# The ordered list of an attention and MLP kernel: lambda on another queue, four weight slices converted later, weight stages filled at its end

## The chip, the cores and the metric

One core of one Trainium2 chip runs the whole program. The metric is device time in microseconds (us) of one execution; 649.22 us is the median of three runs of the kernel before (647.98 to 650.60).

## The reference, cut to what matters

The input is `q`, `k`, `v` of shape 2 x 8 x 768 x 64 and one decay `lam` per head. Attention is linear and decays with distance; it goes through the sequence in blocks and carries a 64 x 64 state per head:

```python
intra = (q_b @ k_b.T * lam**(i-j) for i>=j) @ v_b
inter = (q_b * lam**(i+1)) @ state
state = lam**block * state + (k_b * lam**(block-1-j)).T @ v_b
```

Its output, as 1536 tokens x 512, goes through two MLPs one after the other, each 512 -> 2048 -> 512: the first with h * tanh(softplus(h)) (Mish), the second with max(h, 0) squared.

## The kernel before, in words

Tokens are taken in four chunks t of 384 (N). A *pair* is two heads of one chunk, so there are 16 pairs i = 4t + p. For each pair, TensorE makes the scores (`S`), VectorE masks them with a table of decays (`P1`, `P0`, line L242), ScalarE scales k (`KD`, L203), GpSimd scales q (`QD`, L210), TensorE makes updates and outputs (`U`, `V`), VectorE advances the state (`A`, `A2`, L237), and the result leaves PSUM as a high part (`XH`, ScalarE, L268) and a low part (`XL`, VectorE, L272). The tables (`T`, L179 and L182) are made of `lam` by VectorE at the start. Pairs 2 and 4 to 15 share the PSUM banks X and Y, so the scores of one of them wait for the one ahead to leave.

The MLPs multiply in three passes of a high and a low part (`mm3`, L58 to L60). They run in 128 *steps*, 64 a layer. A step is one chunk t with one slice F of 128 of the hidden width: `m_h` (12 matmuls), the activation `e_a` (L308), its high and low part `e_hi` and `e_lo` (the last is GpSimd's `gl`, L326, once a step), and `m_y` (12 matmuls in layer 0, 9 wider ones in layer 1). Sixteen steps make a phase: four slices, for each of the four chunks.

Each slice F has two weight tiles (io = 0 for `m_h`, 1 for `m_y`), 64 *units* in all, in the order in which they are used, eight a phase. The weights arrive as 64-bit floats and are converted: load of 512 KB (`W`, SP's queue, five raw buffers), `cv_a` on ScalarE (`CA`, L93), three instructions of VectorE in `cv_b` (`CB0`, `CB1`, `CC`: L102, L104, L106), copy of the high part on ScalarE (`CH`, L117), low part on GpSimd (`CL`, L125). A converted tile lies in one of eight slots F mod 8, and `cv_h` refuses to write a slot whose tile has been used fewer than four times.

The attention and steps 0 to 15 (with `m_h(16)`) are not issued in program order. `plan()` writes down operations with an engine, an estimated duration, what they follow, and sometimes a due time; `issue()` runs a list schedule over them: of the operations that can start within 0.25 us of the earliest on an engine, the one with the earliest due time. The order that comes out is fixed at build time; on the chip each engine runs its own list in order and waits only for data. Sixteen units (slices F = 0 to 7) are in this list, and three more loads.

Behind the list the loop runs iterations s = 16 to 127. Each issues `m_h` up to step s+3, `e_c(s+1)`, in odd s one `conv()`, and `y_all(s)`. One `conv()` finishes one unit (`CH`, `CL`), takes the next through `cv_b`, the one after it through `cv_a`, and loads another. `weight()` calls `conv()` until a tile that is asked for is there.

Of the kernel before, what the change touches and what calls it, by code (L numbers as in the profile page):

```python
# [14 lines left out]
RING, RAW = 8, 5  # L15
GROUPS = ((0, 4), (4, 8), (8, 12), (12, 16)), ((0, 4), (4, 8), (8, 12), (12, 16))
AHEAD = 16
# [9 lines left out]
def tile_attn_mlp_mlp(ctx, tc, qkv_in, lam, w1i, w1o, w2i, w2o, out):  # L27
# [354 lines left out]
    ops = {}  # L382
# [13 lines left out]
    def plan():  # L396
        NI = NB * NP
        step_due = lambda s: STEP0 + STEP * s
        op("lam", "ACTq", 0.1, [], lambda: act.dma_start(
            out=lam_b, in_=bass.AP(lam.tensor, lam.offset, [[0, P], [1, H]])))  # L400
        op("lp", "DVE", 0.4, ["lam"], lam_pairs)
        for p in range(NP):
            op(f"T{p}", "DVE", 1.2, ["lp"], lambda p=p: tables(p))
        for i in range(NI):
            a = pr[i]
            j = i - 1
            op(f"kq{i}", "SP", 1.05, [f"kq{j}", f"S{i-4}", f"QD{i-4}"], lambda i=i: load_kq(i))
            op(f"kv{i}", "SP", 1.05, [f"kv{j}", f"kq{i}", f"V{i-4}"], lambda i=i: load_kv(i))
            S_prev = [f"XL{j}", f"A2{j}"] if i > NP else [f"XL{i-3}", f"A2{i-3}"] if i == 3 else []
            if i == NP:  # L410
                S_prev = ["XL2", "A22"]
            op(f"S{i}", "PE", 0.75, [f"kq{i}"] + S_prev + [f"S{j}"], a.scores)
            op(f"KD{i}", "ACT", 0.85, [f"kv{i}", f"T{a.p}"], a.scale_k)
            op(f"QD{i}", "POOL", 1.05, [f"kq{i}", f"T{a.p}", f"V{i-3}"], a.scale_q)
            op(f"U{i}", "PE", 0.4, [f"S{i}", f"KD{i}"], a.updates)
            op(f"P1{i}", "DVE", 0.56, [f"S{i}", f"T{a.p}", f"V{i-2}"], lambda a=a: a.mask(1))
            op(f"P0{i}", "DVE", 0.56, [f"P1{i}"], lambda a=a: a.mask(0))
            chain = [f"U{i}", f"V{i-2}", f"A2{i-2}"] + ([f"A2{i-4}"] if not a.first else [])
            if a.first:
                op(f"AC{i}", "ACT", 0.25, chain, lambda a=a: a.advance(0, a.u[0], (0,)))  # L420
                op(f"AD{i}", "DVE", 0.25, chain, lambda a=a: a.advance(0, a.u[0], (1,)))
                op(f"A{i}", "DVE", 0.56, [f"AC{i}", f"AD{i}"], lambda a=a: a.advance(1, a.u[1]))
            else:
                op(f"A{i}", "DVE", 1.12, chain, lambda a=a: [a.advance(c, a.u[c]) for c in range(2)])
            op(f"V{i}", "PE", 1.35, [f"P0{i}", f"A{i}", f"QD{i}", f"kv{i}"], a.outputs)
            own = step_due(i - 4.7) if i >= NP else None
            op(f"XH{i}", "ACT", 0.5, [f"V{i}"] + ([f"XH{j}"] if a.p else []), a.leave_hi)
            op(f"XL{i}", "DVE", 0.56, [f"XH{i}"], a.leave_lo, own)
            if not a.last:
                op(f"A2{i}", "DVE", 0.57, [f"V{i}", f"XL{i}"], a.leave_state, own)  # L430

        nu = 16
        for u in range(nu):
            F, io = units[u]
            op(f"W{u}", "SP", 1.4, [f"W{u-1}", f"CL{u-RAW}"], lambda u=u: cv_load(u))
            op(f"CA{u}", "ACT", 0.68, [f"W{u}", f"CA{u-1}", f"CC{u-2}"], cv_a)
            op(f"CB0{u}", "DVE", 0.45, [f"CA{u}", f"CC{u-1}"], lambda: cv_b(0))
            op(f"CB1{u}", "DVE", 0.72, [f"CB0{u}"], lambda: cv_b(1))
            op(f"CC{u}", "DVE", 0.72, [f"CB1{u}"], lambda: cv_b(2))
            op(f"CH{u}", "ACT", 0.66, [f"CC{u}", f"CH{u-1}"], cv_h)  # L440
            op(f"CL{u}", "POOL", 1.35, [f"CH{u}", f"CL{u-1}"], cv_l, None if F < 4 else step_due(3 + 1.6 * (u - 8)))
        for u in range(nu, nu + 3):
            op(f"W{u}", "SP", 1.4, [f"W{u-1}", f"CL{u-RAW}"], lambda u=u: cv_load(u), step_due(u - 4))
        unit = {units[u]: u for u in range(nu)}
        for s in range(AHEAD + 1):
            _, _, t, f, st, en = steps[s]
            w, wo = f"CL{unit[f, 0]}", f"CL{unit.get((f, 1))}"
            for a in range(KT):
                dep = [f"XL{NP*t+a}", w, f"MISH{s-2}" if a == 0 else f"HM{s}.{a-1}"]
                op(f"HM{s}.{a}", "PE", 0.53, dep, lambda s=s, a=a: m_h(s, [a]))  # L450
            op(f"MISH{s}", "ACT", 0.5, [f"HM{s}.{KT-1}"], lambda s=s: e_a(s))
            op(f"GH{s}", "ACT", 0.52, [f"MISH{s}", f"GH{s-1}", f"YM{s-2}.{KT-1}"], lambda s=s: e_hi(s))
            op(f"GL{s}", "POOL", 1.05, [f"GH{s}"], lambda s=s: e_lo(s), step_due(s) - 0.6)
            if s == AHEAD:
                break
            for e in range(KT):
                dep = [f"GL{s}", wo, f"YM{s}.{e-1}" if e else f"YM{s-1}.{KT-1}"]
                if st and t:
                    dep.append(f"YD{s-1}.{e}")
                if s == 0:  # L460
                    dep += ["XL0", "A20"] if e < 2 else ["XL1", "A21"]
                    dep += ["XL3", "A23"] if e < 2 else []
                op(f"YM{s}.{e}", "PE", 0.53, dep, lambda s=s, e=e: m_y(s, e), step_due(s) + 0.5 * e)
                if en:
                    op(f"YD{s}.{e}", "ACT", 0.5, [f"YM{s}.{e}"], lambda s=s, e=e: y_out(s, e), step_due(s + 1))

    def issue():
        names = list(ops)
        for n in reversed(names):
            o = ops[n]  # L470
            for a in o.after:
                x = ops[a]
                x.due = min(x.due, o.due - o.dur - LAT - (LAND if x.eng in ("SP", "ACTq") else 0))
        free = {}
        wait = dict(ops)
        trace = []
        while wait:
            cand = {}
            for n, o in wait.items():
                if all(ops[a].end is not None for a in o.after):  # L480
                    r = max([free.get(o.eng, 0.0)] + [
                        ops[a].end + (0 if ops[a].eng == o.eng != "SP" else LAT)
                        + (LAND if ops[a].eng in ("SP", "ACTq") and o.eng != "SP" else 0) for a in o.after
                    ])
                    cand.setdefault(o.eng, []).append((r, o.due, n))
            best = None
            for eng, c in cand.items():
                r0 = min(c)[0]
                pick = min((x for x in c if x[0] <= r0 + SLACK), key=lambda x: (x[1], x[0]))
                if best is None or pick[0] < best[0]:  # L490
                    best = pick
            r, _, n = best
            o = wait.pop(n)
            o.end = free[o.eng] = r + o.dur
            trace.append((r, n, o))
            o.emit()
        if PLAN:
            for r, n, o in trace:
                print(f"{r:7.2f} {o.end:7.2f} {o.eng:4} {n:8} due {o.due:6.1f}")

    with tc.manual_schedule():
        one = const.tile([P, 1], F32, name="one")
        pool.memset(one, 1.0)
        act.activation(gp.tile([P, N], F32, tag="u", name="table", bufs=4)[:, :1], one, AF.Mish)
        make_identity(nc, ident)

        zero = gp.tile([P, N], F32, tag="gl", name="zero")[:, :2 * P]
        dve.memset(zero, 0.0)
        warm = bank("X")
        for _ in range(WARM):  # L510
            pe.matmul(warm[:, :2 * P], lhsT=zero[:, :P], rhs=zero, start=True, stop=True)
        for z in state + mid:
            pool.memset(z, 0.0)
        TAGS = ("y0", "y1"), ("y2", "y3"), ("X", "Y"), ("y0", "y1")
        pr = [Pair(i, TAGS[i] if i < NP else ("X", "Y")) for i in range(NB * NP)]
        plan()
        issue()
        ahead = AHEAD


        wide.append(AHEAD)
        for s in range(AHEAD, len(steps)):
            layer, t, f, _, en = steps[s][1:]
            while ahead + 1 < len(steps) and ahead < s + LOOK:
                ahead += 1
                m_h(ahead)
                e_a(ahead)
            if s + 1 < len(steps):
                e_c(s + 1)
            if s % 2:  # L530
                conv()
            y_all(s)

            for k in range(KT):
                d = s - k - 1
                if d >= 0 and steps[d][1] == 0 and steps[d][5] and phases[steps[d][0]][3] == NF:
                    x_split(steps[d][2], k)
# [50 lines left out]
```

## Time and profile before

| | |
|---|---|
| median of three runs | 649.22 us |
| the profiled execution, its own time | 650.57 us |
| its span, first to last instruction | 648.4 us |
| mean granted TensorE clock | 0.979 |
| TensorE busy | 607.6 us (94%) |
| VectorE busy | 292.3 us (45%) |
| ScalarE busy | 231.4 us (36%) |
| GpSimd busy | 248.2 us (38%) |

Busy time of TensorE is taken from matmuls whose ends are modelled, so 94% is not its peak; whether work flows is better seen from the distance between equal steps. An arrow `<-` at the end of a row of a timeline names what ended the idle time that stands before it. Busy shares over the whole span mix two quite different stretches: the list (to about 146 us) and the loop.

### The profile page before, as it was taken

Reading aid. Unit: us, or ns where it says so; the run is one execution under the profiler, and the core shown is the slowest. Engines: PE = TensorE matmul, PEld = TensorE weight load, DVE = VectorE, ACT = ScalarE, POOL = GpSimd, SP = SyncE. Lnnn points to the kernel's source line nnn. Section 1 sums busy time; section 2 is a strip of 40 time slices with the busy share of each in tenths; the row PEclk is TensorE's granted clock in tenths of the full one; section 3 lists DMA queues with packets and bytes.
Section 4 is the critical chain, followed back from the end, with each engine's and each line's share of the span. In section 5 each row is a group of like instructions: output and inputs, shape, how many; then the busy total and the mean of one; then the engine's idle time right before and its main releaser. Section 6 shows DMA issues by size and latency. Waiting matters only on the chain.

```text
span 648.4 us, 9101 instructions
## 1 busy us (share of the span) xinstructions
PE 607.6 (94%) x3592; PEld 560.3 (86%) x3592; DVE 292.3 (45%) x483; ACT 231.4 (36%) x486; POOL 248.2 (38%) x229
## 2 busy tenths in 40 slices
PE   7888989999999989998999989998999989998997
PEld 6777878999999979998999869987899879987996
DVE  5999974201444334442445534442555445440223
ACT  3465633332333323333344434433233323332111
POOL 2376542121344323343455434334233424434122
PEclk8799989999999989999999979999899999999999
DMA  8865641000011121111222111111211122000112
GB/s 308 294 233 197 215 150 69 1 1 1 16 58 61 62 66 54 58 59 60 66 66 66 38 60 65 55 55 55 67 58 53 51 66 66 33 1 0 50 50 97
DMA packets 15737, 49.86 MB, mean 77 GB/s; under 512 B 1872, under 2 KB 1872, under 8 KB 15696
## 3 DMA queue, kind: packets, MB, share of 16 engines
q1 hardware_dynamic: 15552, 49.29, 22.3%
q8 instruction: 28, 0.46, 0.3%
q14 instruction: 13, 0.11, 0.0%
q10 hardware_dynamic: 144, 0.00, 0.0%
HBM read 46.14 MB, written 3.15 MB: 76 GB/s over the span
## 4 chain that ended last, share of the span: by engine, by line
PE 48%; POOL 3%; issue 3%; DVE 0%; ACT 0%; POOLq 0%; ACTq 0%
PE y L59 9%; PE y L60 8%; PE y L58 8%; PE h L60 4%; PE h L58 4%; PE h L59 4%; PE Y L60 2%; PE Y L58 2%; PE Y L59 2%; POOL w L125 2%; PE X L60 1%; PE X L58 1%; PE X L59 1%; POOL gl L326 1%; DVE y L359 0%
## 5 line engine op out<-in xcount | busy, mean ns | idle before, releaser
L326 POOL TENSOR_TENSOR gl<-g,gh 128x384 fp32r<-128x384 f32 x64 | 67.0, 1046 | 180.8 <-ACT gh L319 175.9
L326 POOL TENSOR_TENSOR gl<-u,gh 128x384 fp32r<-128x384 f32 x64 | 67.7, 1059 | 168.8 <-ACT gh L316 98.4
L359 DVE TENSOR_TENSOR y<-y,y 128x384 f32<-128x384 f32 (+1 forms) x84 | 50.3, 612 | 122.2 <-PE y L60 122.0
L58 PE MATMUL h<-xh,w 128*128 128x384 f32 x288 | 98.3, 341 | 0.1
L60 PE MATMUL h<-xh,w 128*128 128x384 f32 x288 | 97.3, 338 | 0.5 <-POOL w L125 0.5
L59 PE MATMUL h<-xl,w 128*128 128x384 f32 x288 | 96.9, 336 | 0.0
L104 DVE SCALAR_TENSOR_TENSOR raw<-absw,raw 128x512 uint32<-128x512 uint32 x64 | 59.1, 924 | 80.9 <-ACT absw L93 76.6
L308 ACT ACTIVATE u<-h 128x384 f32<-128x384 f32 x72 | 35.4, 492 | 163.9 <-PE h L60 82.9
L125 POOL TENSOR_TENSOR w<-raw,w 128x512 fp32r<-128x512 f32 x64 | 85.7, 1339 | 16.4 <-ACT w L117 16.4
L58 PE MATMUL y<-gh,w 128*128 128x384 f32 x256 | 87.8, 343 | 3.2 <-ACT w L117 3.2
L60 PE MATMUL y<-gh,w 128*128 128x384 f32 x256 | 86.6, 338 | 2.4 <-POOL w L125 2.4
L59 PE MATMUL y<-gl,w 128*128 128x384 f32 x256 | 86.4, 338 | 1.7 <-POOL gl L326 1.7
L59 PE MATMUL y<-w,gh 128*128 128x512 f32 x192 | 77.7, 405 | 5.2 <-POOL w L125 5.2
L58 PE MATMUL y<-w,gh 128*128 128x512 f32 x192 | 76.1, 396 | 6.3 <-ACT w L117 6.3
L60 PE MATMUL y<-w,gl 128*128 128x512 f32 x192 | 77.1, 402 | 0.0
L58 PEld LDWEIGHTS h<-xh,w 128*128 128x128 f32 x288 | 54.4, 189 | 2.6 <-issue 0.3
L59 PEld LDWEIGHTS h<-xl,w 128*128 128x128 f32 x288 | 54.3, 189 | 1.3
L60 PEld LDWEIGHTS h<-xh,w 128*128 128x128 f32 x288 | 54.3, 188 | 1.3 <-POOL w L125 1.3
L106 DVE SCALAR_TENSOR_TENSOR raw<-raw 128x512 uint32<-128x512 uint32 x64 | 52.5, 820 | 2.1
L58 PEld LDWEIGHTS y<-gh,w 128*128 128x128 f32 x256 | 48.6, 190 | 5.2 <-ACT w L117 3.8
L60 PEld LDWEIGHTS y<-gh,w 128*128 128x128 f32 x256 | 48.6, 190 | 3.1 <-POOL w L125 3.1
L59 PEld LDWEIGHTS y<-gl,w 128*128 128x128 f32 x256 | 48.6, 190 | 2.3 <-POOL gl L326 2.3
(86 smaller groups left out, 1005.6 us busy)
## 6 DMA issues: line engine op xcount, KB each, us to landing
raw<-in_w1i_dram SPq DMA_DIRECT2D x16, 512.0 KB, 4.2
raw<-in_w1o_dram SPq DMA_DIRECT2D x16, 512.0 KB, 3.6
raw<-in_w2i_dram SPq DMA_DIRECT2D x16, 512.0 KB, 3.2
raw<-in_w2o_dram SPq DMA_DIRECT2D x16, 512.0 KB, 3.3
kq<-in_qkv_dram SPq DMA_DIRECT2D x16, 384.0 KB, 4.4
kv<-in_qkv_dram SPq DMA_DIRECT2D x16, 384.0 KB, 4.2
out_dram<-y SPq DMA_DIRECT2D x12, 256.0 KB, 2.0
lam_t<-in_lam_dram ACTq DMA_DIRECT2D x1, 4.0 KB, 5.2
```

Of the source, the lines that this page charges most:

```text
L58: pe.matmul(o, lhsT=wh, rhs=xh, start=start, stop=False)
L59: pe.matmul(o, lhsT=wh, rhs=xl, start=False, stop=False)
L60: pe.matmul(o, lhsT=wl, rhs=xh, start=False, stop=stop)
L104: dve.scalar_tensor_tensor(lo, a, 3, lo, ALU.logical_shift_left, ALU.bitwise_or)
L106: dve.scalar_tensor_tensor(lo, hi, 0x80000000, lo, ALU.bitwise_and, ALU.bitwise_or)
L125: pool.tensor_tensor(lo, raw.pop(u).bitcast(F32)[:, :, 0], hi.bitcast(F32), ALU.subtract)
L308: act.activation(u, h, AF.Relu if steps[s][1] else AF.Mish)
L326: pool.tensor_tensor(gl, g, gh.bitcast(F32), ALU.subtract)
L359: dve.tensor_tensor(o, o, y[:, :w], ALU.add)
```

## The change

- `lam` is loaded by SP, as the first of its queue, instead of by ScalarE's queue; in the list kq0 follows it.
- The list's durations become 1.2 for `QD`, 0.55 / 0.95 / 0.95 for the three of VectorE's conversion, 1.4 for `CL`. Due times of `XL` and `A2` and of `CL` (for F >= 4) move.
- `CA` of units 8 to 15 (F = 4 to 7) follows `V` of the pair with the unit's number.
- Five loads instead of three go beyond the sixteen units, and units 16 and 17 are taken through `CA`, `CB0`, `CB1` and `CC` in the list.
- In the loop, `conv()` runs also in iterations 16 and 18.

```diff
--- before.py
+++ after.py
@@ -396,7 +396,7 @@
     def plan():
         NI = NB * NP
         step_due = lambda s: STEP0 + STEP * s
-        op("lam", "ACTq", 0.1, [], lambda: act.dma_start(
+        op("lam", "SP", 0.45, [], lambda: sp.dma_start(
             out=lam_b, in_=bass.AP(lam.tensor, lam.offset, [[0, P], [1, H]])))
         op("lp", "DVE", 0.4, ["lam"], lam_pairs)
         for p in range(NP):
@@ -404,14 +404,14 @@
         for i in range(NI):
             a = pr[i]
             j = i - 1
-            op(f"kq{i}", "SP", 1.05, [f"kq{j}", f"S{i-4}", f"QD{i-4}"], lambda i=i: load_kq(i))
+            op(f"kq{i}", "SP", 1.05, ["lam", f"kq{j}", f"S{i-4}", f"QD{i-4}"], lambda i=i: load_kq(i))
             op(f"kv{i}", "SP", 1.05, [f"kv{j}", f"kq{i}", f"V{i-4}"], lambda i=i: load_kv(i))
             S_prev = [f"XL{j}", f"A2{j}"] if i > NP else [f"XL{i-3}", f"A2{i-3}"] if i == 3 else []
             if i == NP:
                 S_prev = ["XL2", "A22"]
             op(f"S{i}", "PE", 0.75, [f"kq{i}"] + S_prev + [f"S{j}"], a.scores)
             op(f"KD{i}", "ACT", 0.85, [f"kv{i}", f"T{a.p}"], a.scale_k)
-            op(f"QD{i}", "POOL", 1.05, [f"kq{i}", f"T{a.p}", f"V{i-3}"], a.scale_q)
+            op(f"QD{i}", "POOL", 1.2, [f"kq{i}", f"T{a.p}", f"V{i-3}"], a.scale_q)
             op(f"U{i}", "PE", 0.4, [f"S{i}", f"KD{i}"], a.updates)
             op(f"P1{i}", "DVE", 0.56, [f"S{i}", f"T{a.p}", f"V{i-2}"], lambda a=a: a.mask(1))
             op(f"P0{i}", "DVE", 0.56, [f"P1{i}"], lambda a=a: a.mask(0))
@@ -423,7 +423,7 @@
             else:
                 op(f"A{i}", "DVE", 1.12, chain, lambda a=a: [a.advance(c, a.u[c]) for c in range(2)])
             op(f"V{i}", "PE", 1.35, [f"P0{i}", f"A{i}", f"QD{i}", f"kv{i}"], a.outputs)
-            own = step_due(i - 4.7) if i >= NP else None
+            own = step_due(i - 4.2) if i >= NP else None
             op(f"XH{i}", "ACT", 0.5, [f"V{i}"] + ([f"XH{j}"] if a.p else []), a.leave_hi)
             op(f"XL{i}", "DVE", 0.56, [f"XH{i}"], a.leave_lo, own)
             if not a.last:
@@ -433,14 +433,19 @@
         for u in range(nu):
             F, io = units[u]
             op(f"W{u}", "SP", 1.4, [f"W{u-1}", f"CL{u-RAW}"], lambda u=u: cv_load(u))
-            op(f"CA{u}", "ACT", 0.68, [f"W{u}", f"CA{u-1}", f"CC{u-2}"], cv_a)
-            op(f"CB0{u}", "DVE", 0.45, [f"CA{u}", f"CC{u-1}"], lambda: cv_b(0))
-            op(f"CB1{u}", "DVE", 0.72, [f"CB0{u}"], lambda: cv_b(1))
-            op(f"CC{u}", "DVE", 0.72, [f"CB1{u}"], lambda: cv_b(2))
+            op(f"CA{u}", "ACT", 0.68, [f"W{u}", f"CA{u-1}", f"CC{u-2}"] + ([f"V{min(u, NI-1)}"] if F >= 4 else []), cv_a)
+            op(f"CB0{u}", "DVE", 0.55, [f"CA{u}", f"CC{u-1}"], lambda: cv_b(0))
+            op(f"CB1{u}", "DVE", 0.95, [f"CB0{u}"], lambda: cv_b(1))
+            op(f"CC{u}", "DVE", 0.95, [f"CB1{u}"], lambda: cv_b(2))
             op(f"CH{u}", "ACT", 0.66, [f"CC{u}", f"CH{u-1}"], cv_h)
-            op(f"CL{u}", "POOL", 1.35, [f"CH{u}", f"CL{u-1}"], cv_l, None if F < 4 else step_due(3 + 1.6 * (u - 8)))
-        for u in range(nu, nu + 3):
-            op(f"W{u}", "SP", 1.4, [f"W{u-1}", f"CL{u-RAW}"], lambda u=u: cv_load(u), step_due(u - 4))
+            op(f"CL{u}", "POOL", 1.4, [f"CH{u}", f"CL{u-1}"], cv_l, None if F < 4 else step_due(9.5 + 0.8 * (u - 8)))
+        for u in range(nu, nu + 5):
+            op(f"W{u}", "SP", 1.4, [f"W{u-1}", f"CL{u-RAW}"], lambda u=u: cv_load(u), step_due(u - 3))
+        for u in range(nu, nu + 2):
+            op(f"CA{u}", "ACT", 0.68, [f"W{u}", f"CA{u-1}", f"CC{u-2}", f"V{NI-1}"], cv_a)
+            op(f"CB0{u}", "DVE", 0.55, [f"CA{u}", f"CC{u-1}"], lambda: cv_b(0))
+            op(f"CB1{u}", "DVE", 0.95, [f"CB0{u}"], lambda: cv_b(1))
+            op(f"CC{u}", "DVE", 0.95, [f"CB1{u}"], lambda: cv_b(2), step_due(u - 0.5))
         unit = {units[u]: u for u in range(nu)}
         for s in range(AHEAD + 1):
             _, _, t, f, st, en = steps[s]
@@ -470,7 +475,7 @@
             o = ops[n]
             for a in o.after:
                 x = ops[a]
-                x.due = min(x.due, o.due - o.dur - LAT - (LAND if x.eng in ("SP", "ACTq") else 0))
+                x.due = min(x.due, o.due - o.dur - LAT - (LAND if x.eng == "SP" else 0))
         free = {}
         wait = dict(ops)
         trace = []
@@ -480,7 +485,7 @@
                 if all(ops[a].end is not None for a in o.after):
                     r = max([free.get(o.eng, 0.0)] + [
                         ops[a].end + (0 if ops[a].eng == o.eng != "SP" else LAT)
-                        + (LAND if ops[a].eng in ("SP", "ACTq") and o.eng != "SP" else 0) for a in o.after
+                        + (LAND if ops[a].eng == "SP" and o.eng != "SP" else 0) for a in o.after
                     ])
                     cand.setdefault(o.eng, []).append((r, o.due, n))
             best = None
@@ -527,7 +532,7 @@
                 e_a(ahead)
             if s + 1 < len(steps):
                 e_c(s + 1)
-            if s % 2:
+            if s % 2 or s < AHEAD + 4:
                 conv()
             y_all(s)
 
```

## Rows read from the trace of the kernel before

**Rows 1.** Busy us by engine in three stretches: PE, PEld, DVE, ACT, POOL, clock, DMA.
```profile
4.90:57.60 52.70, 44.38 (x429) 37.57 (x428) 48.75 (x99) 25.26 (x57) 27.08 (x22) 0.90 0.77 283
57.60:95.00 37.40, 33.08 (x279) 29.25 (x280) 32.97 (x53) 19.54 (x43) 22.01 (x17) 0.95 0.58 184
95.00:145.70 50.70, 50.68 (x396) 46.93 (x397) 11.79 (x32) 18.11 (x38) 11.81 (x12) 1.00 0.09 30
```

**Rows 2.** Timeline of VectorE up to its first table.
```profile
6.04 0.34 DVE L172 COPY lam_t<-lam_t 64x4 f32<-64x4 f32 x2 [4.92 <-DMA lam_t<-in_lam_dram]
```

**Rows 3.** Waits of TensorE from 150 us on: total, times, longest.
```profile
PE y L58 <- ACT w L117: 9.5, 6, 1.6
PE Y L60 <- POOL w L125: 6.0, 6, 1.0
```

**Rows 4.** Timeline of GpSimd in the loop: start, us, line, idle before.
```profile
153.20 1.01 POOL L326 TENSOR_TENSOR gl<-u,gh 128x384 fp32r<-128x384 f32 x1 [7.51 <-ACT gh L316]
157.36 1.02 POOL L326 TENSOR_TENSOR gl<-u,gh 128x384 fp32r<-128x384 f32 x1 [3.15 <-ACT gh L316]
...
174.97 1.32 POOL L125 TENSOR_TENSOR w<-raw,w 128x512 fp32r<-128x512 f32 x1
...
233.54 1.01 POOL L326 TENSOR_TENSOR gl<-u,gh 128x384 fp32r<-128x384 f32 x1 [3.15 <-ACT gh L316]
...
242.35 1.01 POOL L326 TENSOR_TENSOR gl<-u,gh 128x384 fp32r<-128x384 f32 x1 [6.55 <-ACT gh L316]
...
603.89 1.01 POOL L326 TENSOR_TENSOR gl<-g,gh 128x384 fp32r<-128x384 f32 x1 [5.33 <-ACT gh L319]
608.08 1.01 POOL L326 TENSOR_TENSOR gl<-g,gh 128x384 fp32r<-128x384 f32 x1 [3.18 <-ACT gh L319]
```

**Rows 5.** L58 alone in two of the stretches of rows 2: busy us and count.
```profile
57.60:95.00 37.40, 12.67 (x35) 0.95 0.58 184
95.00:145.70 50.70, 25.21 (x74) 1.00 0.09 30
```

**Rows 6.** Timeline of ScalarE, lines L268 of pairs 7, 11 and 15.
```profile
57.62 0.48 ACT L268 CAST xh<-Y 128x384 fp32r<-128x384 f32 x1 [0.85 <-PE Y L259]
...
94.95 0.48 ACT L268 CAST xh<-Y 128x384 fp32r<-128x384 f32 x1 [3.48 <-PE Y L214]
...
123.03 0.48 ACT L268 CAST xh<-Y 128x384 fp32r<-128x384 f32 x1 [4.43 <-PE Y L259]
```

**Rows 7.** Groups of VectorE from 57.6 to 95 us: count, busy us, mean ns.
```profile
L106 DVE SCALAR_TENSOR_TENSOR raw<-raw 128x512 uint32<-128x512 uint32 x8 | 9.3, 1163 | 0.2
L104 DVE SCALAR_TENSOR_TENSOR raw<-absw,raw 128x512 uint32<-128x512 uint32 x8 | 7.4, 930 | 0.6
L102 DVE TENSOR_SCALAR raw<-raw 128x512 uint32<-128x512 uint32 x7 | 6.1, 868 | 0.1
```

**Rows 8.** Groups of GpSimd in the same stretch.
```profile
L125 POOL TENSOR_TENSOR w<-raw,w 128x512 fp32r<-128x512 f32 x8 | 11.7, 1468 | 6.8 <-ACT w L117 6.8
L210 POOL TENSOR_TENSOR qd<-kq,qs 128x384 f32<-128x384 f32 x5 | 6.7, 1340 | 5.2 <-PE Y L255 3.5 <-issue 1.7
```

**Rows 9.** Timeline of VectorE in a pair without conversion: idle before.
```profile
102.74 0.56 DVE L272 TENSOR_TENSOR xl<-Y,xh 128x384 fp32r<-128x384 f32 x1 [2.47 <-ACT xh L268]
104.89 0.56 DVE L242 TENSOR_TENSOR pm<-Y,dT 128x384 f32<-128x384 f32 x1 [1.59 <-PE Y L223]
```

**Rows 10.** The page: DMA issues, KB of each, median us from issue to landing.
```profile
out_dram<-y SPq DMA_DIRECT2D x12, 256.0 KB, 2.0
lam_t<-in_lam_dram ACTq DMA_DIRECT2D x1, 4.0 KB, 5.2
```

**Rows 11.** Timeline of VectorE, line L104 twice.
```profile
48.64 0.69 DVE L104 SCALAR_TENSOR_TENSOR raw<-absw,raw 128x512 uint32<-128x512 uint32 x1
...
51.60 1.79 DVE L104 SCALAR_TENSOR_TENSOR raw<-absw,raw 128x512 uint32<-128x512 uint32 x1
```

**Rows 12.** Timeline of GpSimd beside the second of them.
```profile
51.55 1.30 POOL L125 TENSOR_TENSOR w<-raw,w 128x512 fp32r<-128x512 f32 x1 [1.33 <-ACT w L117]
```

## The prediction

> **What bounds the kernel now.** I read the busy table by stretches first [rows 1]. From 95 to 145.7 us TensorE is busy 50.68 of 50.7 us at full clock and VectorE only 11.79; from 57.6 to 95 VectorE is busy 32.97 of 37.4 and TensorE has holes; before 57.6 VectorE is busy 48.75 of 52.7, having begun only at 6.04, after 4.92 us idle for lambda [rows 2]. So the list (first scores at 4.90, last `m_h(16)` done at 145.7) is paced by VectorE up to 95 us and by TensorE after it, and the loop behind it by TensorE.
>
> Then I read the waits of TensorE in the loop: six of 1.6 us for the copy of a weight slice (L117), six of 1.0 us for its low part (L125), and a few more of L125 [rows 3]. The timeline of GpSimd places them. One `gl` (L326) is issued per step, number s+1 in iteration s: 153.20 is iteration 16, the first; 603.89 is iteration 116. An undisturbed step is 4.16 us in layer 0 (153.20 to 157.36) and 4.19 in layer 1 (603.89 to 608.08). The 100 steps between took 450.69; 47 x 4.16 + 53 x 4.19 is 417.6. So 33.1 us are lost in the loop, idle and the slow clock behind it together. One such place is 233.54 to 242.35, iteration 35: 8.81 instead of 4.16 [rows 4].
>
> Why iteration 35 follows from the code, and 174.97 confirms it: the first low part of the loop stands 21.77 us behind iteration 16, which is iteration 21 (5 x 4.16 = 20.8, and the `gl` ahead of it). Of phase 2+m, slice j of 8 is number 16+8m+j; `conv()` runs in odd steps and finishes one slice a time, number 16+k in iteration 21+2k. The last of each phase, j=7, is finished in iteration 35+16m, and `y_all(35+16m)` is the first to use it, in the same iteration. Slice j=5 is finished in 31+16m and used by `m_h(35+16m)` one iteration later. That is two waits in each of six phases, as in the rows: 33.1 / 6 = 5.5 us a phase.
>
> **The list, in TensorE's work.** From 95 to 145.7 there are 74 groups of three matmuls [rows 5] of 0.52 us (a step of 4.16 has eight): 38.5 us. The remaining 12.2 are pairs 12 to 15, so 3.05 us a pair. The whole list has 132 groups and 16 pairs: 68.6 + 48.8 = 117.4 us. It takes 145.7 - 4.9 = 140.8, so 23.4 are lost, none after 95. From 57.6 to 95 there are 35 groups and four pairs (XH of pair 7 at 57.62, of pair 11 at 94.95 [rows 6]): 18.2 + 12.2 = 30.4 of 37.4, so 7.0 lost there; 16.4 before.
>
> **The change, part by part.**
> *Weight stages filled.* The list now takes slices 16 and 17 through `cv_b` and loads up to 20; `conv()` also runs in iterations 16 and 18. Slice 16+k is finished in iteration 16+k up to k=3, then in 13+2k. j=7 is ready in iteration 27+16m, eight steps (33 us) before use, j=5 nine. The ring allows it: slot F-8 must have been used four times; for slice 24 (F=12) that is `m_h(28)`, issued in iteration 25, and the new turn comes in 29; for j=7 it is `y_all(31)` against iteration 43. No conversion is added, the same ones run earlier. All 33.1 us go; what is late next is nothing but TensorE itself, whose steps stay at 4.16. In iterations 16 to 19 one slice a step lies beside TensorE: 2.96 us of VectorE (0.87 + 0.93 + 1.16 [rows 7]) and 1.47 + 1.01 of GpSimd [rows 4, 8] in 4.16, so covered; if not, four times under 1 us. Its two extra loads leave from SP behind all loads of kq and kv. Bounds: 33.1, and 0 if the lead is lost.
>
> *Units 8 to 15 behind V8 to V15* (`CA` with `V{u}`; `CL` with later due times). In the 37.4 us before 95, eight units took 8 x 2.96 = 23.7 of VectorE's 32.97. They go to one a pair over pairs 8 to 15. VectorE then needs (32.97 - 23.7) / 4 + 2.96 = 5.3 us a pair; TensorE needs 3.05 + 4.16 = 7.2 for a pair and a step. TensorE becomes the bound, and up to 7.0 come back. In the chain of a pair without conversion VectorE has 2.47 + 1.59 = 4.06 us idle [rows 9], room for one unit. The gate stands only in the list: behind a `CA` on ScalarE stand `KD` and `XH` of the next pairs, behind W13 to W15 on SP the last kq and kv, which have four buffers. I take 5.0 of the 7.0, as about 0.25 us a pair will not fit. Bounds: +7.0 to -3 (the first rival). Units 16 and 17 come behind pair 15, where VectorE is idle.
>
> *Lambda first, on SP.* It took 5.2 us to land although it is 4 KB; a 256 KB store took 2.0 [rows 10]. It was issued beside the kq and kv loads on another queue; now it is ahead of them. Landing 2 to 5.2 us after issue, VectorE starts 0 to 3.2 us earlier; kq0 leaves later by one issue (0.45 in the list's own numbers), which costs at worst that. VectorE was the bound for the next 85 us, so the start is passed on. I take 2.5, near the 2.0 row. The Trainium skill speaks against it: "DMA: Bandwidth & Descriptors", section "Issuing engines are not separate DMA queues", says that DMAs from any engine share the same 16 DMA engines, so that the issuer saves only the time of issue. By that the 2.5 would be about 0 and the time 610; the trace of before, where lambda was in competition and took 5.2, does not contradict it. I count on its place ahead of the other loads.
>
> *Durations and due times* (QD 1.2, CB .55/.95/.95, CL 1.4, XL due at i - 4.2). No instruction changes, only the order; the terms for ACTq that are dropped only follow lambda's move. The rows say 1.34, .87/.93/1.16 and 1.47 [rows 7, 8], so the new figures are nearer. Of the 16.4 us lost before 57.6 I count 1.0 as regained; bounds -3 and +6.
>
> Sum: 33.1 + 5.0 + 2.5 + 1.0 = 41.6. The profiled execution took 650.57 us, so 609.0; it lies 1.35 above the median 649.22, so 607.6 beside the timed runs, and I predict 608.
>
> **Rivals.**
> *A, the list keeps its length.* L104 took 0.69 us alone and 1.79 when it began 0.05 us behind GpSimd's L125 of 1.30 [rows 11, 12]: it stood for it. If each unit's three instructions (at most 3 x 0.69 = 2.1 alone) stand for all of a pair's GpSimd work (1.34 + 1.47 + 1.01 = 3.8), a unit takes 5.9, 1.8 over the room of 4.06. With 7.02 us a pair as now (57.62 or 94.95 to 123.03 [rows 6]: four pairs in 28.08), that is 8.8 x 8 = 71 us from 55.1, so pair 15 at 126 instead of 123: 649.2 - 33.1 + 3 = 619; without the excess 616. The Trainium skill ("SBUF — State Buffer", section "Who interferes with whom") states it as an exclusive lock that blocks the second comer fully; the trace agrees for this instruction. Against A: the mean of 2.96 was measured with GpSimd busy 22.01 of 37.4 [rows 1], as dense as it will be. I expect 614 to 622 for it.
> *B, the list closes up to TensorE.* Then only the start is lost, some 7 us of the 23.4: 16 instead of 8.5 gained, 600. For it: VectorE's load falls most. Against: the pairs remain a serial chain, and before 57.6 the same eight units and eight pairs are done.
> *C, the stages aren't full, or the PE waits for something else there.* Only the list gains: 641; half of it: 625. Against: the six phases fit the counting to the step.
> *D, slower.* A conversion that finds its slot in use is refused and its turn is lost, two steps of the lead each; from four refusals a phase on, the lead of eight is gone, and a slice is forced through at its first use with nothing beside it. That is a load (at least the 2.0 us of half the bytes [rows 10]), two operations of ScalarE (at least 0.48 each, by L268 [rows 6]), 2.96 on VectorE [rows 7] and 1.47 on GpSimd [rows 8]: 7.4 us, where a phase loses 5.5 now. One such slice a phase adds 6 x 1.9 = 11.4, with the list's 8.5 off 652; two, which refusals that pile up would give, 6 x 9.3 = 56, so 697. It decides from one a phase on. Against: every slot that I counted is free at least one turn ahead.
>
> **How the numbers follow.** Forecast 0.60 (602 to 614), A 0.20, B 0.11, C 0.06, D 0.03. The range 597 to 621 holds the forecast, most of A and of B, some 0.87; I leave it there, since the bounds of the list's terms (-6.5 to +16 together, against 8.5 taken) nearly fill it. What a measurement can tell from no change is 0.5%, 3.2 us: faster 0.95, same 0.02, slower 0.03.
>
> **What would show it.** In the loop no wait of TensorE for L117 or L125, and `gl` every 4.16 or 4.19 us from iteration 16 to the end; first low parts in iterations 16, 17, 18, 19, 21. XH of pair 15 about 8 us earlier, near 115, with one L104 per pair from pair 8 on; the loop's start near 137. VectorE's first table near 3.5. Wrong would be: waits at 35+16m that stay, a pair from 8 on that takes over 8 us, or lambda landing at 5 or later.

## The result and the profile after

The changed kernel takes 609.75 us (median of four runs, 605.23 to 610.27) beside 649.91 of the kernel before (four runs). The ratio of the means is 0.9357, with a 95% interval of 0.929 to 0.9424; that of the medians is 0.938. The forecast was 608 in 597 to 621. The profiled execution took 610.27, 40.3 less than that of before.

(The caption of rows 5 means the stretches of rows 1.)

First the busy time by stretches, where the columns are those of [rows 1]; the cuts are moved to pair 7's `XH` (59.1), pair 12's (95.7) and the end of `m_h(16)` (138.5).

```profile
5.50:59.00 53.50, 47.20 (x440) 39.36 (x440) 43.58 (x92) 25.30 (x57) 28.98 (x23) 0.94 0.80 276
59.00:96.00 37.00, 36.90 (x344) 32.46 (x343) 24.30 (x51) 20.60 (x46) 13.81 (x14) 1.00 0.50 153
96.00:138.50 42.50, 42.50 (x321) 39.19 (x320) 22.84 (x41) 18.36 (x36) 14.64 (x13) 1.00 0.18 63
```

The reader is to see the middle line: TensorE is busy 36.90 of 37.0 us where it had 33.08 of 37.4, and VectorE 24.30 where it had 32.97. From pair 7 on the list is paced by TensorE. What TensorE leaves idle is now all in the first line. The list ends at 138.5 instead of 145.7.

Next the timeline of GpSimd in the loop, to be laid beside [rows 4].

```profile
146.03 1.01 POOL L326 TENSOR_TENSOR gl<-u,gh 128x384 fp32r<-128x384 f32 x1 [5.15 <-issue]
147.01 1.30 POOL L125 TENSOR_TENSOR w<-raw,w 128x512 fp32r<-128x512 f32 x1
150.19 1.01 POOL L326 TENSOR_TENSOR gl<-u,gh 128x384 fp32r<-128x384 f32 x1 [1.88 <-issue]
151.16 1.31 POOL L125 TENSOR_TENSOR w<-raw,w 128x512 fp32r<-128x512 f32 x1
...
162.67 1.14 POOL L326 TENSOR_TENSOR gl<-u,gh 128x384 fp32r<-128x384 f32 x1 [1.87 <-issue]
166.83 1.01 POOL L326 TENSOR_TENSOR gl<-u,gh 128x384 fp32r<-128x384 f32 x1 [3.02 <-ACT gh L316]
167.81 1.30 POOL L125 TENSOR_TENSOR w<-raw,w 128x512 fp32r<-128x512 f32 x1
...
233.39 1.01 POOL L326 TENSOR_TENSOR gl<-u,gh 128x384 fp32r<-128x384 f32 x1 [3.01 <-ACT gh L316]
...
237.55 1.01 POOL L326 TENSOR_TENSOR gl<-u,gh 128x384 fp32r<-128x384 f32 x1 [1.88 <-issue]
...
563.37 1.01 POOL L326 TENSOR_TENSOR gl<-g,gh 128x384 fp32r<-128x384 f32 x1 [3.17 <-ACT gh L319]
```

146.03 is iteration 16. A low part (L125) follows in it, in 17 (151.16), 18, 19, not in 20 (162.67), and again in 21 (167.81): the order that was counted. From 233.39 to 237.55 nothing is lost, and the 100 steps from 146.03 to 563.37 take 417.34 us; 417.6 without loss was expected, 450.69 it was. The busy times of these 100 steps, the kernel before first, tell what went:

```profile
153.20:603.89 450.69, 427.58 (x2244) 400.59 (x2243) 187.69 (x281) 156.18 (x324) 174.29 (x156) 0.98 0.16 53
146.03:563.37 417.34, 417.34 (x2244) 396.69 (x2243) 189.21 (x275) 154.61 (x322) 175.41 (x157) 1.00 0.17 57
```

TensorE was idle for 23.1 us, and the same 2244 matmuls were busy 10.2 us longer, at a granted clock of 0.98 instead of 1.00. The waits of TensorE over the whole span are these (total, times, longest):

```profile
PE Y L223 <- DVE xl L272: 1.3, 1, 1.3
PE y L214 <- DVE pm L242: 1.2, 1, 1.2
PE X L516 <- DVE zero L513: 1.2, 1, 1.2
PE Y L259 <- DVE pm L242: 1.0, 1, 1.0
PE h L60 <- POOL w L125: 1.0, 1, 1.0
PE h L59 <- DVE xl L272: 0.8, 2, 0.4
PE h L58 <- ACT w L117: 0.6, 1, 0.6
PE y L223 <- DMA kq<-in_qkv_dram: 0.5, 1, 0.5
```

All of them lie before 60 us; in the loop there is none, where [rows 3] had six of 1.6 and six of 1.0.

The attention, on ScalarE (`XH` of pairs 0, 7, 15), against [rows 6]:

```profile
13.21 0.48 ACT L268 CAST xh<-y 128x384 fp32r<-128x384 f32 x1 [2.90 <-PE y L214]
...
59.10 0.48 ACT L268 CAST xh<-Y 128x384 fp32r<-128x384 f32 x1 [2.21 <-PE Y L259]
...
118.24 0.48 ACT L268 CAST xh<-Y 128x384 fp32r<-128x384 f32 x1 [0.31 <-PE Y L259]
```

Pair 0 leaves at 13.21 (12.92 before), pair 7 at 59.10, 1.5 later than before, pair 15 at 118.24, 4.8 earlier. Ahead of pair 7 the new order has four more groups of `m_h` and `m_y` (30 matmuls of L58 instead of 26), some 2.1 us of TensorE's work at 0.52 a group. The groups of VectorE's conversion over pairs 8 to 15, against [rows 7]:

```profile
L102 DVE TENSOR_SCALAR raw<-raw 128x512 uint32<-128x512 uint32 x7 | 6.7, 954 | 0.1
L104 DVE SCALAR_TENSOR_TENSOR raw<-absw,raw 128x512 uint32<-128x512 uint32 x7 | 5.8, 825 | 0.7
...
L106 DVE SCALAR_TENSOR_TENSOR raw<-raw 128x512 uint32<-128x512 uint32 x7 | 4.9, 704 | 0.2
```

One unit costs 0.95 + 0.83 + 0.70 = 2.48 us there, after 2.96. Last, lambda: VectorE's first instruction on it, and the DMA's row of the page, against [rows 2, 10].

```profile
3.96 0.34 DVE L172 COPY lam_t<-lam_t 64x4 f32<-64x4 f32 x2 [2.83 <-DMA lam_t<-in_lam_dram]
```

```profile
lam_t<-in_lam_dram SPq DMA_DIRECT2D x1, 4.0 KB, 3.2
```

It lands in 3.2 us instead of 5.2, and VectorE starts 2.1 earlier. But pair 0 leaves no earlier. That the forecast had otherwise, and e4 and e9 to e13 ask why. The forecast also had pair 15 near 115, where 118.24 was measured.

### The profile page after: what moved, and what is told of

It reads as the page before. It is cut to its first block, busy times and chain, and to the rows that moved or that the text cites. A ratio compares the mean times of both kernels' runs of the same rounds, so it can differ in the third digit from the quotient of the medians.

```text
span 608.3 us, 9108 instructions
## 1 busy us (share of the span) xinstructions
PE 595.9 (98%) x3592; PEld 553.6 (91%) x3592; DVE 292.5 (48%) x483; ACT 231.7 (38%) x486; POOL 246.8 (41%) x229
## 4 chain that ended last, share of the span: by engine, by line
PE 91%; DVE 3%; issue 3%; POOL 1%; DMA 1%; ACT 0%; SPq 0%; POOLq 0%; DVEq 0%; ACTq 0%
PE y L58 14%; PE y L60 14%; PE y L59 14%; PE h L58 8%; PE h L59 8%; PE h L60 8%; PE Y L58 3%; PE X L58 3%; PE X L60 3%; PE Y L60 3%; PE Y L59 3%; PE X L59 3%; PE Y L255 1%; PE X L223 1%; PE Y L259 1%
## 5 line engine op out<-in xcount | busy, mean ns | idle before, releaser
L58 PE MATMUL h<-xh,w 128*128 128x384 f32 x288 | 98.3, 341 | 0.6 <-ACT w L117 0.6
L104 DVE SCALAR_TENSOR_TENSOR raw<-absw,raw 128x512 uint32<-128x512 uint32 x64 | 60.5, 946 | 66.2 <-ACT absw L93 61.8
L58 PE MATMUL y<-gh,w 128*128 128x384 f32 x256 | 87.4, 341 | 0.0
L125 POOL TENSOR_TENSOR w<-raw,w 128x512 fp32r<-128x512 f32 x64 | 86.3, 1349 | 0.5 <-ACT w L117 0.5
L59 PE MATMUL y<-w,gh 128*128 128x512 f32 x192 | 75.8, 395 | 0.0
L58 PE MATMUL y<-w,gh 128*128 128x512 f32 x192 | 74.6, 389 | 0.0
L58 PEld LDWEIGHTS h<-xh,w 128*128 128x128 f32 x288 | 54.2, 188 | 3.7 <-issue 1.2
L58 PEld LDWEIGHTS y<-gh,w 128*128 128x128 f32 x256 | 48.0, 188 | 1.6 <-issue 0.2
L102 DVE TENSOR_SCALAR raw<-raw 128x512 uint32<-128x512 uint32 x64 | 49.1, 768 | 0.2
```

Of the source, the lines that this page charges most:

```text
L58: pe.matmul(o, lhsT=wh, rhs=xh, start=start, stop=False)
L59: pe.matmul(o, lhsT=wh, rhs=xl, start=False, stop=False)
L102: dve.tensor_scalar(lo, lo, 29, None, op0=ALU.logical_shift_right)
L104: dve.scalar_tensor_tensor(lo, a, 3, lo, ALU.logical_shift_left, ALU.bitwise_or)
L125: pool.tensor_tensor(lo, raw.pop(u).bitcast(F32)[:, :, 0], hi.bitcast(F32), ALU.subtract)
```

## The experiments

| kernel | median us | ratio to before, 95% | iteration 16 at us |
|---|---|---|---|
| the change | 609.75 | 0.9357 (0.929 to 0.9424) | 146.03 |
| e1, two more turns of conv only | 616.13 | 0.9471 (0.944 to 0.9502) | 151.16 |
| e2, one more turn only | 616.46 | 0.9479 (0.9452 to 0.9505) | 152.29 |
| e3, filling undone | 643.80 | 0.9898 (0.9866 to 0.9931) | 143.33 |
| e4, lambda back | 608.22 | 0.9355 (0.9329 to 0.938) | 144.77 |
| e6, gate undone | 611.66 | 0.9413 (0.9373 to 0.9453) | 148.36 |
| e7, old durations | 609.04 | 0.9377 (0.9356 to 0.9398) | 144.82 |
| e8, gate and two turns only | 609.29 | 0.938 (0.9362 to 0.9397) | 145.38 |
| e9, weights behind kv3 | 608.34 | 0.9379 (0.935 to 0.9408) | 143.20 |
| e10, six warm-up matmuls | 606.60 | 0.9356 (0.9325 to 0.9386) | 142.43 |
| e11, two behind the first scores | 606.19 | 0.934 (0.9309 to 0.9371) | 142.32 |
| e12, e9 and six warm-up matmuls | 608.38 | 0.9373 (0.9344 to 0.9402) | 143.45 |
| e13, e11 with lambda back | 608.96 | 0.9361 (0.9339 to 0.9383) | 145.30 |

The last column is the start of the `gl` of iteration 16 in the profiled execution (153.20 before). The kernel before took 650.8, 649.1, 649.0 and 650.5 us beside the four sets (e1 to e4, e6 to e9, e10 to e12, e13), so medians of different sets are best compared by the ratio.

**e1 and e2: is it the lead, and how much of it?**

```diff
-            if s % 2:
+            if s % 2 or s < AHEAD + 4:    # e1
+            if s % 2 or s == AHEAD:       # e2
```

> The kernel before with one line of the change: conv() runs also in iterations 16 and 18; the list is as it was. Slice 16+k is then finished in iteration 17+2k instead of 21+2k, so the last slice of a phase is ready four steps ahead of its first use. Theory (the loop lost its 33 us because the last slice of each phase was finished in the very iteration that uses it, and any lead of a whole iteration ends that): all 33 us go, about 617 us, no wait of TensorE for L117 or L125 behind iteration 16. Rival (the stages must be filled by the list, with slices 16 and 17 converted there): waits remain in the first phases or all, 625 to 649 us.

> The kernel before with conv() in iteration 16 as well and nothing else: slice 16+k is finished in iteration 19+2k, a lead of two steps instead of none. Theory: a step is 4.16 us and the copy, gl and low part together take about 3, so two steps are enough: about 617 us again, no waits. Rival (a lead must cover more, as the eight steps of the change do): some of the twelve waits stay, 625 us or more.

616.1 and 616.5, and in neither is there a wait of TensorE behind iteration 16. From iteration 16 to the end of the span e1 and e2 take 461.8 us each, the change 462.3, the kernel before 495.2. So one extra turn, a lead of two steps instead of none, is worth the whole 33 us; the eight steps that the change builds up are more than is needed, and the filling in the list adds nothing to it. A lead of one step was not tried. The rival that waits would stay is out.

**e3: filling undone.** Three loads behind unit 15, no conversion of units 16 and 17, `conv()` in odd iterations.

```diff
-        for u in range(nu, nu + 5): ... step_due(u - 3)
-        for u in range(nu, nu + 2): ... CA, CB0, CB1, CC
+        for u in range(nu, nu + 3): ... step_due(u - 4)
-            if s % 2 or s < AHEAD + 4:
+            if s % 2:
```

> The changed kernel with the filling undone: three loads beyond the sixteen units as before, no conversion of units 16 and 17 in the list, conv() in odd iterations only. Theory (list and loop are independent): the loop loses its 33 us again and the list keeps its 7.2, 642.5 us, with the waits of 1.6 and 1.0 us back in iterations 35+16m and 32+16m. Rival (the filling is what shortens the list too): 649 us.

643.8, and the waits in the loop (total, times, longest) are those of [rows 3] again:

```profile
PE y L58 <- ACT w L117: 9.5, 6, 1.6
PE Y L60 <- POOL w L125: 6.3, 6, 1.3
```

List and loop are independent. The list alone keeps 7.0 us by the medians of this set (650.8), 4.5 to 8.7 by the interval of the ratio.

**e6, e7, e8: what in the list does it?** e6 takes the gate of `CA` and the later due times of `CL` out of the change, e7 its durations and due times of `XL`; e8 adds only the gate and e1's line to the kernel before.

```diff
- ... + ([f"V{min(u, NI-1)}"] if F >= 4 else []), cv_a)    # e6 without, e8 with
- step_due(9.5 + 0.8 * (u - 8))                            # e6: 3 + 1.6 * (u - 8)
- "POOL", 1.2 / "DVE", 0.55, 0.95, 0.95 / "POOL", 1.4      # e7: 1.05 / .45, .72, .72 / 1.35
- step_due(i - 4.2)                                        # e7: i - 4.7
```

> The changed kernel with the units 8 to 15 released: CA no longer follows V of a pair, CL has its old due times; the durations and everything else stay. Theory (the list's gain is the spreading of these eight conversions over eight pairs): they crowd into four pairs again, VectorE is full up to about 92 us, and the list's 7 us are gone, 615 to 617 us. Rival (the more realistic durations alone make a list that TensorE paces): 610 us.

> The changed kernel with the old durations (QD 1.05, CB .45/.72/.72, CL 1.35) and the old due time of XL and A2 (i - 4.7); gate and filling stay. Theory (the durations are worth little, the gate does it): 609 to 612 us. Rival: 614 us or more. As predicted (1.0 us): 610.8.

> The kernel before with two edits of the change only: conv() also in iterations 16 and 18, and the gate of CA with the later due times of CL. Lambda, durations and the filling by the list stay as before. Theory (two terms make the gain, 33 in the loop and 7 in the list): 609 to 611 us, the same as the whole change. Rival (each part of the change is needed): 613 to 616 us.

e7 and e8 came out as the theory had it: 609.0 and 609.3, so the gate with one line in the loop does what the whole change does, within intervals that overlap. e6 did not: 611.7 instead of 615 to 617, though above the rival's 610. Its interval overlaps the change's, so its times alone do not show that the gate adds anything to the durations. Its busy times from 59 to 96 us:

```profile
59.00:96.00 37.00, 35.07 (x319) 30.87 (x316) 33.52 (x58) 21.92 (x48) 20.55 (x16) 1.00 0.65 206
```

VectorE is crowded again (33.52 of 37), but TensorE is idle only 1.9 us there, not the 4.3 of the kernel before (37.4 - 33.08 [rows 1]). Without the gate the longer durations alone spread units 8 to 15: their last low part falls at 99.39 us instead of 91.55 in the kernel before (in the change at 124.22). So gate and durations are two ways to the same end, and their gains do not add: from the profiles the durations without the gate bring 4.8 us (e6, 153.20 to 148.36), the gate without the durations 7.8 (e8, to 145.38), both 7.2. These are single profiles; three of the same list (before, e1 and e2) lie 2.0 apart, at 151.16 to 153.20.

**e4: lambda back on ScalarE's queue.** `act.dma_start` for `sp.dma_start`, kq0 no longer behind it; the rest of the change stays, and the order on VectorE and GpSimd is the same.

> The changed kernel with lambda on ScalarE's queue as before. As predicted (lambda first is worth 2.5 us): 612.3 us, the loop starting 2.5 us later than in the changed kernel (146.0 for the gl of iteration 16). Theory after the result (lambda's 2 us on VectorE are lost again, since kq and kv leave one issue later and the first pairs then wait for their loads): within 1 us of the changed kernel, 609 to 611, first table near 6, pair 0 leaving near 12.9.

608.2, ratio 0.9355 against 0.9357: just below the 609 to 611 of the theory after the result, far from the 612.3 of the forecast; pair 0 left at 12.56. Lambda first brought nothing that can be measured. The reason I gave there is at most a small part of it, though, as e3 shows by chance. Its start is built in the same order as the change's, and its pair 0 left at 10.79. TensorE's timeline from 5 us, the change first:

```profile
5.50 1.65 PE L223 MATMUL y<-kq 64*128 64x128 f32 x12 [0.53 <-DMA kq<-in_qkv_dram]
8.35 0.69 PE L214 MATMUL y<-kv 128*64 128x64 f32 x8 [1.20 <-DVE pm L242]
8.97 1.65 PE L223 MATMUL y<-kq 64*128 64x128 f32 x12
10.55 0.69 PE L259 MATMUL y<-pm,kv 128*64 128x128 f32 x4
11.03 0.64 PE L255 MATMUL y<-qd,mid 128*64 128x128 f32 x4
```

```profile
5.22 1.65 PE L223 MATMUL y<-kq 64*128 64x128 f32 x12 [0.25 <-DMA kq<-in_qkv_dram]
8.06 0.45 PE L214 MATMUL y<-kv 128*64 128x64 f32 x8 [1.20 <-ACT kv L203]
8.45 0.94 PE L223 MATMUL y<-kq 64*128 64x128 f32 x12
9.31 0.44 PE L259 MATMUL y<-pm,kv 128*64 128x128 f32 x4
9.58 0.39 PE L255 MATMUL y<-qd,mid 128*64 128x128 f32 x4
```

Each line is a group of equal matmuls (start, duration, line, tile). The first scores (L223) take 1.65 us in both, at half rate. In e3 the next twelve take 0.94 and the groups of the outputs (L259, L255) 0.44 and 0.39; in the change 1.65, 0.69 and 0.64, until 13.5 us. From one group of outputs to the next it is 0.43 us in the change (11.03 to 11.46) and 0.22 in e3 (9.58 to 9.80), half the rate, as with TensorE's clock at 1.2 instead of 2.4 GHz. The granted clock that the view gives for the stretch does not show it (1.00, the first number behind the last count):

```profile
5.00:15.00 10.00, 8.31 (x85) 1.00 1.03 406
```

The trace's first record of the clock stands at 13.6 us in the change and at 6.8 in e3, and the view gives what lies ahead of the first record as 1.00. In the kernel before the records begin at 6.6 us, and 10 to 15 us reads 0.66.

The kq landing in the change was at most 0.3 us later than in e3 (5.50 against 5.22). So in this execution half rate on TensorE (2.4 us at pair 0, 13.21 against 10.79) ate what lambda's 2.1 us on VectorE gave. With lambda late the half rate is there too. The first outputs of the kernel before, then of e2, whose list is the same:

```profile
10.14 0.70 PE L259 MATMUL y<-pm,kv 128*64 128x128 f32 x4 [0.76 <-DVE pm L242]
10.21 0.69 PE L259 MATMUL y<-pm,kv 128*64 128x128 f32 x4
```

In e2 TensorE is at half rate from the first scores on and waits for no mask, and pair 0 leaves at 12.89; in e6, at half rate too but with lambda first, at 12.97. So at half rate an early table is of no use: TensorE is the bound. Whether other executions of the change lose as much is not shown. One of its four timed runs took 605.23, with a mean granted clock of 1.000, but it left no profile.

**e9 and e12: are the landings the bound?** Every weight load follows kv3 in the list; e12 has six warm-up matmuls as well.

```diff
-            op(f"W{u}", "SP", 1.4, [f"W{u-1}", ...
+            op(f"W{u}", "SP", 1.4, ["kv3", f"W{u-1}", ...
```

> The changed kernel with every weight load behind kv3 on SP's queue, so the first two weight loads (512 KB each, 1.3 us each at the 400 GB/s that the start shows) no longer stand among the loads of the first four pairs. Theory (with lambda early, the start of the list is bound by the landing of kq and kv): the first pairs leave 1 to 2.5 us earlier and the whole takes 607 to 609 us. Rival (the start is bound by the chain of the pairs, or by unit 0, which now lands later): no change or up to 2 us slower, 610 to 612 us.

> The kernel with every weight load behind kv3 and six warm-up matmuls: both edits of the start together, on the changed kernel. If the start is bound by clock and landings at once: 604 to 606 us, pair 0 leaving near 10.7, pair 7 near 56. If neither is worth anything that lasts: 608 to 610.

e9 looked like a hit by its median, 608.3, and pair 0 left at 10.69. But its scores ran at full rate like e3's, and its ratio is 0.9379, not below the change's. One wait of its profile tells what the edit did:

```profile
PE h L58 <- ACT w L117: 3.2, 1, 3.2
```

The first `m_h` waits 3.2 us for slice 0, which now lands later. e12 has the same wait and stands against e10 in the same set: with the clock alike at the start (pair 0 at 11.25 and 10.98), pair 2 leaves earlier (17.72 against 18.50), pair 3 later (27.73 against 26.35), and the median is 1.8 us higher (608.4 against 606.6; the intervals of the ratios overlap). Moving the loads does not pay. That the landings of kq and kv hold up pair 2 is not excluded by it, since unit 0's conversion has moved behind pair 2's masks on VectorE as well.

**e10, e11, e13: is it TensorE's clock?** e10 has `WARM = 6`. e11 has two more of the warm-up matmuls (`hot[0](2)`) behind the scores of pair 0, where TensorE stands idle, and e13 is e11 with lambda back on ScalarE's queue.

```diff
-            op(f"S{i}", "PE", 0.75, ..., a.scores)
+            op(f"S{i}", "PE", 0.75, ..., a.scores if i else lambda a=a: [a.scores(), hot[0](2)])
```

> The changed kernel with six warm-up matmuls ahead of the first scores instead of four (two of 0.94 us more at the half rate of the first four, or half of that). In the changed kernel's profile the first two pairs run at half rate up to 13.5 us (scores 1.65 us, outputs 0.64 a group), in two other profiles with the same start at full rate from 8 us on (0.94, 0.39), and pair 0 then leaves at 10.7 instead of 13.2. Theory (lambda first is paid back by TensorE's clock, since kq0 lands 0.3 to 0.5 us behind the end of the warm-up): with TensorE kept busy up to kq0 and beyond, pair 0 leaves before 11.5 in most executions and the median falls to 606 to 608. Rival (the start is bound by the landings, the clock costs nothing that remains): 609 to 611.

> The changed kernel with two more warm-up matmuls right behind the scores of pair 0, into the same bank, where TensorE stands idle for 1.2 us until kv0 is scaled. Theory of the clock: pair 0 leaves before 11.5 and the median is 606 to 608; if the two run at half rate they delay the first updates by up to 0.7 us. Rival: 609 to 611.

> The kernel with two warm-up matmuls behind the first scores (606.2 us, pair 0 leaving at 10.7), and lambda on ScalarE's queue as before the change. Theory (once TensorE's clock holds through the first pairs, lambda first is worth what VectorE gains, some 2 us): 607.5 to 609 us, first table near 5.7 to 6.0, pair 0 leaving between 11.5 and 12.5. Rival (lambda's place is worth nothing either way): 605.5 to 607.

606.6 and 606.2, as the theory had it; ten of the twelve executions took 604.97 to 607.70. By the ratios neither can be told from the change (0.9356 and 0.934 against 0.9357); what the clock did is shown by the profiles alone. In eight of the ten profiles with four warm-up matmuls, the kernel before among them, pair 0's outputs ran wholly or in part at half rate (the first group of L259 0.56 to 0.70 us); in e3 and e9 and in all four with two matmuls more (e10 to e13) they took 0.44. The start of TensorE in e11:

```profile
5.24 1.36 PE L223 MATMUL y<-kq 64*128 64x128 f32 x12 [0.28 <-DMA kq<-in_qkv_dram]
6.53 1.13 PE L519 MATMUL X<-zero 128*128 128x256 f32 x4
7.98 0.45 PE L214 MATMUL y<-kv 128*64 128x64 f32 x8 [0.32 <-issue]
8.36 0.94 PE L223 MATMUL y<-kq 64*128 64x128 f32 x12
9.23 0.44 PE L259 MATMUL y<-pm,kv 128*64 128x128 f32 x4
```

The two extra matmuls (6.53, four records) fill the gap, the updates wait 0.32 us instead of 1.20, and the outputs run at full rate; pair 0 leaves at 10.70. In e10 the gap of 1.20 stays, and what the longer warm-up fills is the time until kq0 is there; its first scores run at full rate already (0.94). e13 holds the clock there too (its scores 0.94), but stands and waits for VectorE's mask, whose table comes later (waited for: 0.81 us):

```profile
8.41 0.94 PE L223 MATMUL y<-kq 64*128 64x128 f32 x12
10.16 0.44 PE L259 MATMUL y<-pm,kv 128*64 128x128 f32 x4 [0.81 <-DVE pm L242]
```

It takes 609.0, and the `gl` of iteration 16 starts at 145.30 instead of e11's 142.32, 3.0 later. Pair 0 leaves 1.4 later (12.14) and pair 2 1.65 later (19.89 against 18.24). The rest comes behind pair 2, where the two executions differ in the granted clock as well (27 to 31 us, e11 first):

```profile
27.00:31.00 4.00, 3.60 (x42) 2.86 (x40) 3.76 (x9) 2.86 (x8) 2.36 (x3) 1.00 0.84 276
27.00:31.00 4.00, 3.78 (x37) 3.12 (x33) 2.06 (x6) 2.29 (x5) 2.37 (x2) 0.62 0.75 248
```

So once the clock holds at the start, lambda first is worth some 1.6 us in these two profiles; whether the rest is its doing is open. By the ratios it is 0.2% (0.9361 and 0.934, intervals that overlap): the times do not show it.

e11 has the lowest median of the study. Its interval (0.9309 to 0.9371) overlaps that of the change (0.929 to 0.9424), so the times do not show that it beats it; its six runs lie between 604.97 and 607.70, where one of the change's four did, and its loop starts 3.7 us earlier in the profile (142.32 against 146.03), of which pair 2 has 2.4 already (18.24 against 20.67).

## Why the prediction was right

- *The loop, 33.1 us.* Right in place, size and mechanism: 450.69 - 417.34 = 33.35, no wait left, the low parts in the iterations that were counted. It was "idle and the slow clock behind it together", as written: 23.1 of idle TensorE and 10.2 of longer busy time. e1 to e3 show that it is the lead alone. The prediction did not ask how much lead is needed; two steps are enough.
- *Units 8 to 15, 5.0 of 7.0 us.* Right in kind, undersized: TensorE idles 0.1 us from 59 to 96, where it idled 4.3, and by the prediction's own count of work (0.52 a group, 3.05 a pair) 6.6 us came back behind pair 7. The 0.25 us a pair that "will not fit" did fit; a unit cost 2.48 us there, not 2.96. Pairs 8 to 15 took (118.24 - 59.10) / 8 = 7.39 us each, near the 7.2 of TensorE's work.
- *Lambda, 2.5 us.* The start of VectorE came as predicted (3.96; 3.5 was named). What that is worth with the clock held stays between 1.6 us at pair 2 and 3.0 at the loop's start (e13 against e11). The step that failed is "VectorE was the bound for the next 85 us, so the start is passed on": in the first pairs TensorE, at half rate, was the bound. In the profiled execution pair 0 left 0.3 us later than before, so nothing of the term shows. The Trainium skill ("DMA: Bandwidth & Descriptors", section "Issuing engines are not separate DMA queues") has the DMAs of all issuing engines interleave on the same 16 DMA engines, so that another issuer saves only the time of issue. By that the term would be about 0, as it came out, but not for that reason: lambda did land sooner, in 3.0 to 3.2 us in the eight profiles with it first on SP's queue, in 4.7 to 5.3 in the six with it on ScalarE's. Its place ahead of the large loads, on which the prediction counted, is another matter than its issuer.
- *Durations, 1.0 us.* Nothing that shows beside the gate (e7 609.0); without it 4.8 (e6). I had added them as independent terms.
- *Sum of the list:* 8.5 predicted, 7.2 measured, 10.9 with the clock held at the start (e11, 153.20 to 142.32). That 7.2 is near 8.5 is in part luck: behind pair 7 came 6.6 where 5.0 was taken, ahead of it, by the same count of work, 0.6 where lambda and the durations were to bring 3.5, and the two errors partly cancel.
- *Rivals.* A: no; a pair took 7.39 us, not 8.8. The lock of the Trainium skill ("SBUF — State Buffer", section "Who interferes with whom") is seen on single instructions [rows 11, 12]. The mean of L104 went down to 0.83; GpSimd was less dense, as the prediction argued against A, busy 13.81 of 37.0 us from 59 to 96 instead of 22.01 of 37.4. B came half: from pair 7 on TensorE is the bound, but of the list's 133.0 us (5.5 to 138.5) against 117.4 of work 15.6 are still lost, nearly all ahead of 59 us. Of C and D no sign appeared.

## What to carry to other kernels

Count in which iteration a prefetched tile is finished and in which it is first used: if the last of a group is finished in the very step that uses it, a steady rate makes the same stall in every group, and one extra turn of the prefetch at the start removes all of them. Work that is due late and is put as early as possible can crowd the engine that paces the early stage; here a gate or longer, measured durations in the list cured the same thing, and their gains did not add. An engine that starts earlier passes its gain on only as far as the next engine is not the bound, and at the start of a kernel TensorE's clock can make it so.

## What the runs showed of the hardware that I had not expected

- The same instructions in the same order at the start ran at half rate up to 13.5 us in one execution (the change: scores 1.65 us) and at full rate from 8 us in another (e3: 0.94), with 1.2 us of idle TensorE ahead in both. What decides between the two is open. With two matmuls more, ahead of the first scores (e10, e12) or in the gap behind them (e11, e13), all four profiles show the full rate.
- The granted clock read 1.00 in a stretch where matmuls ran at half rate, because the trace has no record of the clock ahead of its first change (13.6 us in the change) and the view gives such time as 1.00. At the beginning of a span the durations of equal matmuls are the surer sign.
